# First x tiles on two load queues, and a new order of work within the first attention layer

## The chip, the cores and the metric

The kernel runs on one core of a Trainium2 chip. The metric is the device time of one execution in microseconds (us). The core has five engines that run their own instruction queues in order and meet only at semaphores: PE (TensorE, matrix multiply), DVE (VectorE), ACT (ScalarE), POOL (GpSimd) and SP (SyncE, which here only issues DMA transfers). ACT and POOL issue some transfers too.

## What is computed

Four blocks in a row on x, 2048 rows of 512 bf16 numbers: linear attention with 32 heads (layers 0 and 2) and a gated feed-forward block of width 1792 (layers 1 and 3), both with the same weights at their second use.

```python
def _A_ref(x, wqkv, wo):                      # H = 32, Dh = 16
    q, k, v = split_heads(x @ wqkv)
    phi = lambda t: jnp.where(t > 0, t + 1, jnp.exp(t)) + 1e-6
    pq, pk = phi(q), phi(k)
    kv = jnp.einsum("bhsd,bhse->bhde", pk, v)
    z = jnp.einsum("bhsd->bhd", pk)
    num = jnp.einsum("bhqd,bhde->bhqe", pq, kv)
    den = jnp.einsum("bhqd,bhd->bhq", pq, z)[..., None] + 1e-6
    return merge_heads(num / den) @ wo

def _B_ref(x, w_gate, w_up, w_down):
    return (silu(x @ w_gate) * (x @ w_up)) @ w_down

x = x + _A_ref(layernorm(x), wqkv, wo)
x = x + _B_ref(layernorm(x), w_gate, w_up, w_down)
x = x + _A_ref(layernorm(x), wqkv, wo)
x = x + _B_ref(layernorm(x), w_gate, w_up, w_down)
```

## The kernel before

The rows are cut into 16 tiles of 128 rows (x0 to x15), four to a group. Everything stays in SBUF. The order of the work is written out by hand: PROGRAM is the order of the steps, and with it the order of PE's instructions, and ORDER holds one list of operation names for each of the other engines. The class Prog keeps account of who wrote and read which buffer and sets the waits (`sync`, L65). A name is layer, step, tile, a dot and the kind of operation: `0x4.apply` is the application of the layer norm to tile 4 in layer 0, `0k0.exp` an operation of the projection of tile 0 to k. A number at the end counts operations of the same name on one engine (`0d3.pqn`, `0d3.pqn1`). The sets ON_ACT and ON_POOL say for some operations which engine does them.

The steps of layer 0, in the letters of PROGRAM:

- `S` is a matmul on zeros, without use for the result, which occupies PE until the first tile is there (L1250).
- `0x` (`ln`, L561) normalizes a tile. For most tiles DVE takes the statistics (stats L574, aggr L576); for tiles 2, 3, 6 and 14 ACT does (stats L581, sq L589) and POOL negates the mean (negm L593). Then vpe (L605, on POOL or DVE) and pow (L609, POOL) give 1/sqrt(var + eps); for tiles 11 and 14 ACT does that (rsl, rse, L599 and L601). The apply is on DVE (L620), or on ACT (L616), for which POOL first makes nmr (L613).
- `0t` (L632) transposes tiles 0 to 3 on PE, and ACT or DVE copies them out of PSUM (xT, L648, L651). Tiles 4 to 15 are transposed by DMA from SP's queue (xT, L629), one after the other.
- `0k` and `0q` project a tile (k) or a group (q, in four parts) with four matmuls of 512 columns, followed by phi (L660): ACT's exp (L664), for some also ACT's id1 (L667), and DVE's ts (L669) and phi (L673 where there is an id1, else L676).
- `0g` accumulates the products of k and the normalized x over all tiles in four pinned PSUM banks; `0z` sums k with matmuls of one column; `0d` forms the denominators and scales q by their reciprocals (pqn, L854). These are spread over a tile by a DMA transpose (rT, L844) of what ACT has repeated (rex, rep). In group 2 PE does it (`0r`).
- `0v` and `0m` form the matrices GT that `0w` multiplies with the scaled q, adding the result to x; after each `0w` DVE and others begin the layer norm of layer 1 for that tile.
- In layer 1, `1u` is a pair of projections (gate and up) with one SiLU, its product is named h. The Wd.tw operations between them subtract blocks of the down weights from each other.

PSUM has eight banks of 512 numbers per partition; a step takes the one that was used longest ago (`bank`, L448), if it isn't pinned.

All loads are issued by `dma` (L511). SP issues the first four tiles singly (ldx), then pairs of tiles (ldy), Wq (ldq) and Wv (ldv); ACT issues the two halves of Wk (ldk). The weights of later steps follow from POOL.

Of the kernel before, what the change touches and what calls it, by code (L numbers as in the profile page):

```python
# [192 lines left out]
1u001 1u006 1u012 1u011 0d33 1u004 1u005 1u013 1u003 1u008 1u002 1u010 1u113 1u101 1u009 0w13 1u110 0w14 1u104
1u105 0w15 0w12 1p01 1u102 1u107 1u112 1p05 1p06 1u103 1u108 1p07 1p02 1p04 1p03 1u111 1u100 1u109 1u106 1u213
1u206 1p11 1p15 1u208 1p16 1u210 1p17 1p12 1u207 1p14 1u203 1p13 2k0 2k1 1u303 1u209 2k2 1u204 1u212 2k4 1u205
1u202 1u201 1u211 1u302 1u309 2q01 2k3 1u200 1u310 1u306 1u313 1u308 1u301 1u304 2k6 2q10 1p21 2k5 1u305 1p26 1u307
1p27 1u300 1p22 1p25 1u311 1p24 1u312 1p23 1p31 1p35 2k7 1p36 1p33 1p37 2k11 2q02 1p34 1p32 2q12 2q00 2k9 2g11 2g2
2k10 2k8 2g7 2k15 2k14 2g10 2q11 2k13 2k12 2g9 2q31 2q20 2q21 2g13 2q13 2q03 2s 2g3 2g0 2d02 2d01 2d00 2d03 2g14
2d21 2g15 2q23 2d11 2g1 2q22 2g12 2g6 2d13 2d23 2g8 2g5 2d10 2d12 2g4 2d20 2d22 2q33 2v 2r1 2m3 2m1 2m2 2m0 2w3 2w2
2w0 2q32 2w1 2w6 2d31 2q30 2w4 2w8 2w7 2d32 2w10 2w9 2d33 2w11 2d30 2w5 3u001 3u010 3u004 3u008 3u005 3u000 3u002  # L200
2w12 2w15 3u009 2w14 2w13 3u011 3y105 3y101 3u012 3u003 3u006 3u007 3y111 3u112 3y115 3y106 3u105 3y116 3y102 3y107
3u013 3y104 3y103 3y121 3y112 3y117 3p01 3p05 3y113 3p06 3y125 3y114 3p02 3y131 3y126 3p07 3y132 3u106 3y136 3y122
# [15 lines left out]
0q20.exp 0q20.id1 0d0.rex2 0d1.ln 0G0.evac 0G2.evac 0G3.evac 0d1.rex1 0q30.exp 0d1.rex 0d2.ln 0d2.rxs 0q31.exp
0M0.evac 0q33.id1 0M1.evac 0M3.evac 0q33.exp 0d1.rex2 0d1.rex3 1x1.sq 1x2.sq 1x3.sq 1x2.apply 1x0.sq 0q32.id1
0q32.exp 1x0.apply 1x5.sq 1x4.sq 1x6.sq 1x11.sq 1x5.apply 1x7.sq 1u000.silu 1u007.silu 1x10.sq 1x8.sq 1u001.silu  # L220
1x9.sq 1u006.silu 1u012.silu 1u011.silu 1u004.silu 0d3.rep 0d3.rep1 1u005.silu 1u013.silu 1u003.silu 1u008.silu
1x11.apply 1u002.silu 1x9.apply 0d3.rep2 0d3.rep3 1u010.silu 1u113.silu 1u101.silu 1u009.silu 1u110.silu 1x13.sq
1u104.silu 1x14.sq 1x13.apply 1u105.silu 1x15.sq 1x12.sq 1u102.silu 1x15.apply 1x12.apply 1u107.silu 1u112.silu
1u103.silu 1u108.silu 2x2.sq 2x3.sq 1u111.tanh 2x1.sq 2x0.sq 1u100.tanh 2x2.apply 2x3.apply 1u109.tanh 2x1.apply
1u106.tanh 1u213.tanh 1u206.tanh 1u208.tanh 1u210.tanh 1u207.tanh 2x7.sq 1u203.tanh 2x6.sq 2x7.apply 2k0.exp 2x4.sq
1u303.tanh 2k1.exp 2x5.sq 1u209.tanh 2x6.apply 2k2.exp 2x5.apply 1u204.tanh 1u212.tanh 2k4.id1 2k4.exp 1u205.tanh
# [1143 lines left out]
```

## Time and profile before

| | |
|---|---|
| median of 3 runs | 410.11 us (409.76 to 410.12) |
| the profiled execution | 410.09 us, of which the span from the first to the last instruction is 408.3 us |
| PE busy | 397.8 us (97%) |
| DVE busy | 322.6 us (79%) |
| ACT busy | 245.2 us (60%) |
| POOL busy | 135.7 us (33%) |
| loads and stores | 23.29 MB moved, DMA engines busy 24% of the span |

Times in the profile are counted from the start of the span. The engines' names stand as above; SPq, ACTq and POOLq are the DMA-issuing instructions of an engine, PEld the weight loads of PE. An entry L469 is the line of the code that recorded the operation; all matmuls are recorded at one line, so they are told apart by what they read. Matmuls are pipelined: a group of them lasts longer than the distance to the start of the next.

### The profile page before, as it was taken

To read this page: it belongs to the slowest core of one execution; us is meant where nothing else is said; L and a number is where in the kernel's file an instruction comes from. 1 tells how busy PE (TensorE), PEld (TensorE's weight loads), DVE (VectorE), ACT (ScalarE), POOL (GpSimd) and SP (SyncE) were. 2 spreads that over 40 slices of the span, in tenths; PEclk is the share of its full clock that TensorE was granted. 3 is DMA by queue.
4 is the path that set the end of the run, shared out by engine and by line. 5 is a ranking of instruction groups with operands and counts; after the bars stand their busy time and mean duration, and the time that the engine had idled before them with its cause. 6 is when DMAs were issued, how large, how long until landed. Compare 5 with 4: busy or idle time off the path is not lost.

```text
span 408.3 us, 7311 instructions
## 1 busy us (share of the span) xinstructions
PE 397.8 (97%) x2673; PEld 244.2 (60%) x2714; DVE 322.6 (79%) x750; ACT 245.2 (60%) x492; POOL 135.7 (33%) x281
## 2 busy tenths in 40 slices
...
GB/s 274 141 101 270 197 52 90 195 60 46 51 2 40 13 1 53 0 2 0 2 27 30 50 2 61 83 65 81 49 27 0 44 12 0 53 2 0 2 54 51
DMA packets 53188, 23.29 MB, mean 57 GB/s; under 512 B 46432, under 2 KB 52064, under 8 KB 53152
## 3 DMA queue, kind: packets, MB, share of 16 engines
...
q10 hardware_dynamic: 544, 0.52, 0.4%
...
## 4 chain that ended last, share of the span: by engine, by line
PE 85%; ACT 6%; DVE 4%; DMA 2%; POOL 2%; issue 1%; SPq 0%; DVEq 0%; ACTq 0%
PE pb L469 85%; ACT etmp L664 1%; DMA RT<-rrep 1%; DMA X<-in_A_x_dram 1%; DVE X L884 1%; DVE pq L872 1%; ACT GT L758 1%; POOL rstd L609 1%; POOL Wqkv L975 1%; ACT tht L916 1%; DVE pk L676 0%; ACT pk L667 0%; ACT xnA L589 0%; ACT xnT L648 0%; POOL nmr L613 0%
## 5 line engine op out<-in xcount | busy, mean ns | idle before, releaser
L469 PE MATMUL pb<-xnT,Wu 128*128 128x512 bf16 (+1 forms) x383 | 95.0, 362 | 0.3
L469 PE MATMUL pb<-xnT,Wg 128*128 128x512 bf16 (+1 forms) x370 | 92.4, 362 | 0.9
L469 PEld LDWEIGHTS pb<-xnT,Wu 128*128 128x128 bf16 x388 | 38.0, 98 | 39.4
L469 PEld LDWEIGHTS pb<-xnT,Wg 128*128 128x128 bf16 x388 | 37.9, 98 | 34.3 <-DVE X L884 0.3
L918 DVE TENSOR_TENSOR hT<-tht,pb 128x512 bf16<-128x512 f32 x50 | 34.0, 683 | 22.1 <-PE pb L469 11.5
L664 ACT ACTIVATE etmp<-pb 128x512 bf16<-128x512 f32 x64 | 37.0, 597 | 14.4 <-PE pb L469 12.2
L916 ACT ACTIVATE tht<-pb 128x512 f32<-128x512 f32 x50 | 29.5, 594 | 26.8 <-PE pb L469 24.9
L1044 POOL TENSOR_TENSOR hT<-pq 128x256 bf16<-128x256 f32 x24 | 18.5, 778 | 76.9 <-ACT pq L1034 76.7
L907 ACT ACTIVATE tht<-pb 128x512 f32<-128x512 f32 x32 | 19.0, 595 | 35.4 <-PE pb L469 33.3
L469 PE MATMUL pb<-Wd,hT 128*128 128x256 bf16 x336 | 40.1, 273 | 0.0
L1049 ACT ACTIVATE pq<-pb 128x512 f32<-128x512 f32 x45 | 25.9, 595 | 22.6 <-PE pb L469 19.9
L593 POOL TENSOR_SCALAR mv<-sums 128x1 f32<-128x1 f32 x52 | 13.4, 267 | 75.8 <-DVE sums L1241 55.1
L609 POOL TENSOR_TENSOR rstd<-vpe,negh 128x1 f32<-128x1 f32 x62 | 36.0, 586 | 7.3 <-DVE vpe L605 4.2
L469 PEld LDWEIGHTS pb<-Wd,hT 128*128 128x128 bf16 x336 | 32.9, 98 | 5.7
L469 PE MATMUL pb<-Wqkv,xnT 128*128 128x512 bf16 x125 | 30.5, 379 | 2.7 <-ACT xnT L648 2.6
L1039 DVE TENSOR_TENSOR pq<-pb,pq 128x512 f32<-128x512 f32 x45 | 30.2, 684 | 3.3 <-ACT pq L1049 1.4
L469 PE MATMUL pb<-GT,pq 128*128 128x512 bf16 x125 | 30.1, 379 | 1.6 <-ACT GT L758 1.3
L469 PE MATMUL pb<-xnT,Wqkv 128*128 128x512 bf16 x122 | 30.9, 379 | 0.3
L469 PE MATMUL pb<-pk,xnA 128*128 128x512 bf16 x123 | 30.7, 378 | 0.3
L669 DVE TENSOR_SCALAR etmp<-etmp 128x512 bf16<-128x512 bf16 x64 | 18.4, 291 | 14.4 <-ACT etmp L664 14.0
L909 DVE SCALAR_TENSOR_TENSOR tht<-tht,pb 128x512 f32<-128x512 f32 x32 | 21.8, 684 | 6.1 <-ACT tht L907 5.9
L589 ACT ACTIVATE etmp<-X,sums 128x512 bf16<-128x512 bf16 x32 | 22.9, 716 | 4.1 <-DVE X L884 4.0
...
## 6 DMA issues: line engine op xcount, KB each, us to landing
out_dram<-pq SPq DMA_DIRECT2D x16, 128.0 KB, 1.8
...
Wd<-in_B_w_down_dram POOLq DMA_DIRECT2D x7, 256.0 KB, 4.5
X<-in_A_x_dram SPq DMA_DIRECT2D x6, 256.0 KB, 4.7
...
X<-in_A_x_dram SPq DMA_DIRECT2D x4, 128.0 KB, 3.5
Wqkv<-in_A_wqkv_dram ACTq DMA_DIRECT2D x2, 256.0 KB, 3.6
```

The costliest lines, as they stand in the source:

```text
L469: return op("pe", lambda e: e.matmul(o_ap, lhsT=lhsT, rhs=rhs, start=start, stop=stop, skip_group_check=skip), r=r, w=w, n=n)
L589: op("act", lambda a: a.activation(out=sq_ap, in_=X[:, t, :], func=ACT.Square, scale=-float(D), bias=sums[:, t:t + 1], accum_out=mv[:, t, ...
L609: op("pool", lambda p: p.tensor_tensor(out=rstd[:, t:t + 1], in0=vpe[:, t:t + 1], in1=negh[:], op=ALU.pow), r=[f"vp{t}", "negh"], w=[f"rs{ ...
L664: exps.append(op("act", lambda a: a.activation(out=etmp[e][:], in_=PB[pb], func=ACT.Exp), r=[f"pb{pb}"], w=[f"e{e}"], after=silus, kind="e ...
L669: op("dve", lambda v: v.tensor_scalar(out=etmp[e][:], in0=etmp[e][:], scalar1=1.0, scalar2=1e-6, op0=ALU.min, op1=ALU.add), r=[f"e{e}"], w ...
L907: op("act", lambda e: e.activation(out=tht[a][:], in_=PB[pg], func=ACT.Tanh, scale=0.5), r=[f"pb{pg}"], w=[f"th{a}"], kind="tanh")
L909: op("dve", lambda v: v.scalar_tensor_tensor(out=tht[a][:], in0=tht[a][:], scalar=1.0, in1=PB[pg], op0=ALU.add, op1=ALU.mult), r=[f"pb{pg} ...
L916: silus.append(op("act", lambda e: e.activation(out=tht[a][:], in_=PB[pg], func=ACT.Silu), r=[f"pb{pg}"], w=[f"th{a}"], after=exps, kind=" ...
L918: op("dve", lambda v: v.tensor_tensor(out=hT[h][:, j, :], in0=tht[a][:], in1=PB[pu], op=ALU.mult), r=[f"pb{pu}", f"th{a}"], w=hk, kind="h")
L1039: op("dve", lambda v: v.tensor_tensor(out=c, in0=PB[b], in1=c, op=ALU.add), r=[f"pb{b}", k], w=[k], kind="ca")
L1044: lambda e: e.tensor_tensor(out=hT[h][:, jj, o:o + 256], in0=c[:, 0:256], in1=c[:, 256:512], op=ALU.mult),
L1049: op("act", lambda e: e.activation(out=gs_tmp[3 * f + n], in_=PB[pb], func=ACT.Copy), r=pk_, w=[f"gt{3 * f + n}"], kind="cp")
```

## The change

Three things are changed. First, the loads of x1, x2 and Wk0 change queues: SP issues x0, x3 and Wk0, ACT issues x2, x1 and Wk1, in these orders. Second, the orders of all engines are written anew as far as the end of layer 0's attention, and with them some operations change engines: the applies of tiles 1 and 15 go from DVE to ACT and that of tile 4 from ACT to DVE; vpe of tile 8 goes from POOL to DVE; id1 of 0k8, 0k13 and 0q21 is left out (their phi takes the form without it) and 0q13 has one; G0 and G3 are evacuated by DVE instead of ACT, G1 by ACT instead of DVE. Third, one of the multiplies of group 3 (0d3, tile 1 of the group) goes from DVE to POOL, which stands where layer 1 has begun. After that the orders are as before. Other keys that leave ON_ACT are of operations that don't occur; `3s` in the code isn't in the set.

```diff
 PROGRAM = """
-S S S ... S 0t0 S 0k0 S S
-0t2 0t1 0t3 0k2 0k1 0k3 0q00 0q03 0g0 0g2 0g1 0g3 0k4 0k9 0q01 0k10 0k5 0g4 0z2 0g9 0z1 0k6 0z3 0z10 0q12 0k7 0k13
-0k15 0k14 0g5 0z5 0q13 0g6 0z6 0z9 0z13 0q11 0z14 0k8 0k11 0z7 0q02 0q23 0z0 0k12 0z11 0z4 0z15 0g8 0q22 0z12 0z8
-0q21 0d03 0d00 0d02 0d01 0g10 0q10 0d13 0g12 0g14 0g11 0q20 0d10 0d11 0d21 0g15 0d12 0g7 0d23 0g13 0d22 0q30 0d20
-0v 0q31 0m0 0q33 0m2 0m3 0m1 0w1 0w2 0w3 0d30 0r2 0w0 0w5 0q32 0w4 0d31
+S S S ... S S 0t0 0t2 0k0
+0t3 S 0k2 0t1 0k3 S 0k1 0q03 0q00 0g2 0g3 0g0 0k4 0g1 0k9 0q01 0k10 0k5 0g4 0z2 0g9 0z1 0k6 0z3 0z10 0q12 0k7 0k13
+0k15 0k14 0g5 0z5 0q13 0g6 0z9 0q11 0z14 0z13 0k8 0z6 0k11 0z7 0q02 0q23 0k12 0z4 0z11 0z15 0g8 0q22 0z12 0z8 0z0 0q21
+0d03 0d02 0d01 0d00 0g10 0g12 0q10 0d13 0d21 0g11 0q20 0d10 0d11 0g14 0g15 0d12 0g7 0d23 0g13 0d22 0d20 0q30 0v 0q31
+0m0 0q33 0m3 0m2 0m1 0w1 0w2 0w3 0d30 0r2 0w0 0w5 0w4 0q32 0d31
...
     "act": """
-i.ldk i.ldk1 0x2.stats 0x2.sq 0x3.stats 0x3.sq 0t0.xT 0k0.exp 0t2.xT 0t1.xT 0k0.id1 0x4.apply 0k2.exp 0k1.exp 0x6.stats 0k3.exp
-0q00.id1 0q00.exp 0x5.apply 0q03.exp 0x6.sq 0x14.stats 0x14.sq 0x7.apply 0k4.id1 0k4.exp 0k9.exp 0x14.rsl 0q01.exp
+i.ldx1 i.ldx i.ldk 0x2.stats 0x2.sq 0x3.stats 0x3.sq 0t0.xT 0t2.xT 0x1.apply 0k0.exp 0k0.id1 0t1.xT 0k2.exp 0k3.exp
+0x6.stats 0x14.stats 0k1.exp 0x6.sq 0x14.sq 0q03.exp 0q00.exp 0q00.id1 0x5.apply 0k4.exp 0k4.id1 0x7.apply 0x14.rsl
+0x14.rse 0k9.exp 0q01.exp 0x15.apply 0k10.exp 0k10.id1 0k5.exp 0x11.rsl 0x14.apply 0x8.apply 0k6.exp 0x11.rse 0q12.id1
...
     "dve": """
-i.c 0x0.stats 0x0.aggr 0x0.apply 0x1.stats 0x2.vpe 0x1.aggr 0x1.vpe 0x3.vpe 0x2.apply 0x4.stats 0x1.apply 0x3.apply
-0x4.aggr 0x9.stats 0x10.stats 0x9.aggr 0t3.xT 0k0.ts 0x5.stats 0k0.phi 0x9.apply 0x10.aggr 0x5.aggr 0k2.ts 0x7.stats
-0k1.ts 0k2.phi 0x10.apply 0k3.ts 0k1.phi 0k3.phi 0q00.ts 0x7.aggr 0x13.stats 0q00.phi 0x13.aggr 0q03.ts 0x15.stats
-0q03.phi 0x15.aggr 0x6.apply 0x11.stats 0x13.apply 0x8.stats 0k4.ts 0x15.apply 0k9.ts 0k4.phi 0k9.phi 0q01.ts
+i.c 0x0.stats 0x0.aggr 0x1.stats 0x2.vpe 0x0.apply 0x1.aggr 0x1.vpe 0x2.apply 0x3.vpe 0x4.stats 0x3.apply 0x9.stats
+0x4.aggr 0x9.aggr 0t3.xT 0x7.stats 0x10.stats 0k0.ts 0x5.stats 0k0.phi 0k2.ts 0x5.aggr 0k3.ts 0x4.apply 0x10.aggr
+0k2.phi 0k3.phi 0x7.aggr 0x9.apply 0k1.ts 0k1.phi 0x10.apply 0q03.ts 0x15.stats 0q03.phi 0x13.stats 0q00.ts 0x15.aggr
+0x13.aggr 0x6.apply 0q00.phi 0k4.ts 0x8.stats 0x11.stats 0x8.aggr 0k9.ts 0k4.phi 0q01.ts 0x11.aggr 0x8.vpe 0k9.phi
...
-1u010.h 1u113.h Wd.tw5 Wd.tw7 1x10.apply 1u101.h 0d3.pqn2 1x8.apply 0d3.pqn3 1u009.h 1h0.sb 0w13.res 1h0.sa 1h0.sb3
...
+0d3.pqn1 1u010.h 1u113.h Wd.tw5 Wd.tw7 1x10.apply 1u101.h 0d3.pqn2 1x8.apply 1u009.h 1h0.sb 0w13.res 1h0.sa 1h0.sb3
...
     "pool": """
-i.c5 i.c i.c2 i.c6 i.c1 i.c4 i.c3 i.c7 i.c8 i.c9 0x0.vpe 0x0.pow 0x2.negm 0x3.negm 0x2.pow 0x1.pow 0x3.pow 0x4.vpe
+i.c7 i.c i.c5 i.c8 i.c4 i.c6 0x0.vpe 0x2.negm 0x0.pow i.c1 0x2.pow 0x3.negm 0x1.pow 0x3.pow 0x1.nmr i.c2 i.c3 0x4.vpe
...
-1x9.pow 1x11.pow 1x9.nmr 1x10.vpe 1x10.negm 1x10.pow 1x8.vpe 1x11.nmr 1x8.pow Wd.tw2 1x8.negm Wd.tw3 Wd.tw Wd.tw1
+1x9.pow 1x11.pow 1x9.nmr 1x10.vpe 1x10.negm 1x10.pow 1x8.vpe 1x11.nmr 1x8.pow Wd.tw2 1x8.negm Wd.tw3 Wd.tw 0d3.pqn
...
     "sp": """
-i.ldx i.ldx2 i.ldx3 i.ldx1 i.ldy i.ldy2 i.ldy3 i.ldy1 i.ldq i.ldy5 i.ldy4 i.ldv 0x4.xT 0x9.xT 0x10.xT
-0x5.xT 0x6.xT 0x7.xT 0x15.xT 0x13.xT 0x14.xT 0x8.xT 0x11.xT 0x12.xT 0d0.rT1 0d0.rT 0d0.rT3 0d0.rT2 0d1.rT1 0d1.rT
+i.ldx i.ldx1 i.ldk i.ldy i.ldy2 i.ldy3 i.ldy1 i.ldq i.ldy5 i.ldy4 i.ldv 0x4.xT 0x9.xT 0x10.xT 0x5.xT 0x6.xT 0x7.xT
+0x15.xT 0x13.xT 0x14.xT 0x8.xT 0x12.xT 0x11.xT 0d0.rT1 0d0.rT 0d0.rT3 0d0.rT2 0d1.rT1 0d1.rT 0d1.rT2 0d1.rT3 1x1.xT
...
 ON_POOL = set("""
-0d0.2 0d0.3 2d0.2 2d0.3
+0d0.2 0d0.3 0d3.1 2d0.2 2d0.3
 """.split())
...
         for t in range(TG):
-            dma("sp", X[:, t, :], x2d[t * P:(t + 1) * P, :], w=[f"x{t}"], kind="ldx")
+            dma("act" if f"0a{t}" in ON_ACT else "sp", X[:, t, :], x2d[t * P:(t + 1) * P, :], w=[f"x{t}"], kind="ldx")
         for c in range(2):
-            dma("act", Wqkv[:, 2 * c:2 * c + 2, D:2 * D], wq3[:, 2 * c:2 * c + 2, D:2 * D], w=[f"Wk{c}"], kind="ldk")
+            dma("sp" if f"0b{c}" in ON_ACT else "act", Wqkv[:, 2 * c:2 * c + 2, D:2 * D], wq3[:, 2 * c:2 * c + 2, D:2 * D], w=[f"Wk{c}"], kind="ldk")
```

In ON_ACT after the change stand, of the keys that count here, 0a1, 0a2, 0b0, 0p8, 0q13, 0x1, 0x15, 0G1; 0G0, 0G3, 0k8, 0k13, 0q21, 0x4 are gone.

## Rows read from the trace of the kernel before

**Rows 1.** The page: busy us, share of the span, instructions.
```profile
PE 397.8 (97%) x2673; PEld 244.2 (60%) x2714; DVE 322.6 (79%) x750; ACT 245.2 (60%) x492; POOL 135.7 (33%) x281
```

**Rows 2.** Waits of PE, whole span: us in total, times, longest.
```profile
PE pb L469 <- ACT xnT L648: 2.6, 2, 2.2
PE pb L469 <- ACT GT L758: 1.3, 2, 0.8
```

**Rows 3.** Timeline of PE: start us, us, operation, count, idle before and releaser.
```profile
5.74 0.40 PE L643 MATMUL pb<-ident,xnA 128*128 128x128 bf16 x4
...
8.38 0.81 PE L469 MATMUL pb<-Wqkv,xnT 128*128 128x512 bf16 x3 [2.19 <-ACT xnT L648]
...
9.13 0.83 PE L643 MATMUL pb<-ident,xnA 128*128 128x128 bf16 x12
10.36 2.76 PE L469 MATMUL pb<-Wqkv,xnT 128*128 128x512 bf16 x12 [0.40 <-ACT xnT L648]
...
18.14 1.89 PE L469 MATMUL pb<-Wqkv,xnT 128*128 128x512 bf16 x8
...
55.73 2.60 PE L469 MATMUL pb<-GT,pq 128*128 128x512 bf16 x11 [0.47 <-ACT GT L758]
```

**Rows 4.** Timeline of ACT, 4 to 12 us.
```profile
4.51 0.63 ACT L581 ACTIVATE xnA<-X 128x512 bf16<-128x512 bf16 x1 [2.44 <-DMA X<-in_A_x_dram]
...
7.44 0.57 ACT L648 ACTIVATE xnT<-pb 128x512 bf16<-128x512 bf16 x1
9.22 0.60 ACT L664 ACTIVATE etmp<-pb 128x512 bf16<-128x512 f32 x1 [1.21 <-PE pb L469]
...
10.67 0.70 ACT L667 ACTIVATE pk<-pb,onep 128x512 bf16<-128x512 f32 x1
11.24 0.83 ACT L616 ACTIVATE xnA<-X,nmr,rstd 128x512 bf16<-128x512 bf16 x1
```

**Rows 5.** Timeline: the first DMA issues of SP and of ACT.
```profile
0.79 3.83 SPq L512 DMA_DIRECT2D X<-in_A_x_dram  x8
0.81 0.96 ACTq L512 DMA_DIRECT2D Wqkv<-in_A_wqkv_dram  x2
```

**Rows 6.** DMA, stretches of single issues (x0, Wk0, x2, x1; tiles 4, 9): us to landing.
```profile
X<-in_A_x_dram SPq DMA_DIRECT2D x1, 128.0 KB, 2.6
Wqkv<-in_A_wqkv_dram ACTq DMA_DIRECT2D x1, 256.0 KB, 3.3
...
X<-in_A_x_dram SPq DMA_DIRECT2D x1, 128.0 KB, 3.2
...
X<-in_A_x_dram SPq DMA_DIRECT2D x1, 128.0 KB, 3.8
...
xnT<-xnA SPq DMA_TRANSPOSE x1, 3.4
...
xnT<-xnA SPq DMA_TRANSPOSE x2, 3.0
```

**Rows 7.** Timeline of DVE, 12 to 14 us.
```profile
11.98 0.40 DVE L620 TENSOR_SCALAR xnA<-X,mv,rstd 128x512 bf16<-128x512 bf16 x1
...
13.61 0.68 DVE L676 SCALAR_TENSOR_TENSOR pk<-pb,etmp 128x512 bf16<-128x512 f32 x1
```

**Rows 8.** Windows, 10.4 to 26 us: busy PE, PEld, DVE, ACT, POOL; clock, DMA.
```profile
10.40:26.00 15.60, 15.47 (x85) 7.32 (x88) 15.23 (x46) 15.19 (x33) 8.43 (x24) 1.00 0.57 126
```

**Rows 9.** Timeline, 83 to 97 us, where layer 1 has begun.
```profile
83.18 5.46 POOL L553 TENSOR_TENSOR Td<-Wd,Td 128x512 bf16<-128x512 bf16 x5
...
90.30 3.40 SPq L844 DMA_TRANSPOSE RT<-rrep  x2
90.42 0.75 DVE L854 TENSOR_TENSOR pq<-pq,RT 128x512 bf16<-128x512 bf16 x2
...
96.12 1.03 PE L469 MATMUL pb<-xnT,Wg 128*128 128x512 bf16 x4
```

**Rows 10.** DMA, the RT transpose issued at 90.30: us to landing.
```profile
RT<-rrep SPq DMA_TRANSPOSE x1, 3.2
```

More of the change, by code (lines that the diff above doesn't have):

```diff
@@ L193 @@
[L193 to L202, printed above, removed]
@@ L209 @@
+3y336 3y335 3p26 3y332 3y327 3y337 3p22 3y323 3u313 3p27 3y333 3y324 3y341 3y345 3p24 3y346 3y342 3y334 3y347 3p23
+3y343 3y344 3p31 3p32 3p35 3p36 3p33 3p37 3p34
 """
@@ L218 @@
[L218 to L226, printed above, removed]
-1u202.tanh 1u201.tanh 1u211.tanh 1u302.tanh 1u309.tanh 2q01.exp 2q01.id1 2k3.id1 2k3.exp 1u200.tanh 1u310.tanh
@@ L249 @@
+3y333.sih 3y346.cp 3y334.sih 3y347.cp 3y342.sih 3y347.sih 3y344.sih 3y343.sih
 """,
     "dve": """
[L251 to L254 removed]
```

164 lines of the change are left out of this document (88 added, 76 removed).

## The prediction, made before the changed kernel was run

> **What bounds the kernel now.** I read the page's engine shares first, then PE's waits, then the timeline of the first 26 us engine by engine, and the issues of the first loads. PE is busy 397.8 of 408.3 us, 97% [rows 1], so only time in which PE has nothing to do can be won. Once it works, PE waits for another engine's data almost nowhere: 2.6 us in two waits for a transposed tile that ACT copies out of PSUM, and 1.3 us in two for GT [rows 2]; one of these two GT waits lies at the end of the first attention layer and one in layer 2. The reader should see in rows 3 that both tile waits are at the very start: PE transposes tile 0 at 5.74, stands still for 2.19 us, begins 0k0 at 8.38, and stands still for another 0.40 us before 0k2 at 10.36. From there on one group follows the other without a gap: twelve 512-column matmuls take 2.76, eight take 1.89, so four cost 0.865 us. So this kernel is a start of some 10 us and then PE at its rate; a microsecond saved in the start lasts to the end if no later stage makes PE wait, and whatever PE waits later is lost.
>
> What sets 8.38: PE waits for ACT's 0t0.xT at 7.44 [rows 4]. PE had finished the transposes before 6.2; ACT was not free. Its queue holds 0x2.stats, 0x2.sq, 0x3.stats, 0x3.sq ahead of that copy, begun at 4.51, after 2.44 us of waiting for tile x2 [rows 4]. So x2's landing sets 0k0: 8.38 - 4.51 = 3.87 us from landing to first projection. x2 is the second transfer on SP's queue: eight issues take 3.83 us there, 0.48 each [rows 5], so it goes out at 1.27, and lands 3.2 us later [rows 6].
>
> **The change, part by part.** *Loads.* SP now issues x0, x3, Wk0 and ACT x2, x1, Wk1. x2 becomes the first transfer of its queue, 128 KB at 0.81 instead of 1.27. What such a one takes is bounded by two rows: x0, first on SP with 128 KB, 2.6 us; Wk0, first on ACT with 256 KB, 3.3 us [rows 6]. So x2 lands between 3.4 and 4.1, and I take 3.4 because x0 is the same size in the same place. That is 1.1 us earlier (0.4 at the other end). x3 and x1 become second in their queues, like x2 before: about 4.5 (1.27 + 3.2); as fourth transfer x1 landed at 6.0 (3.8 us after its issue at 2.2 [rows 6]). x3 is in time for ACT, which reaches it 1.5 us after x2. The price is Wk: Wk0 and Wk1 now stand where x3 and x1 stood, with the same bytes ahead of each queue's end, so they land by about 6.0. 0k0 needs them at 7.3; the cover is 1.3 us and I cost this at nothing. Later transfers on SP go one issue earlier with the same bytes ahead and I leave them where they were. The Trainium skill speaks against this part: "DMA: Bandwidth & Descriptors", section "Rules for kernel authors", says that spreading DMAs over issuing engines brings no bandwidth, since they share the same DMA engines, and only saves issue time. By that rule alone x2 would gain its issue slot and no more.
>
> *ACT's start.* The four statistics operations still stand ahead of 0t0.xT, so 0k0 comes 3.87 us after x2: 3.4 + 3.9 = 7.3 instead of 8.38, a gain of 1.1. 0x0.apply moves behind 0x1.stats and 0x2.vpe on DVE, and on POOL 0x2.negm goes ahead of 0x0.pow; this delays 0x0.apply, and with it the transposes that began at 5.74 [rows 3], by some 0.3 us, to about 6.0, and ACT is free for the copy at 3.4 + 2.9 = 6.3, so this costs nothing (cover 0.2 to 0.3 us).
>
> *The order on PE.* 0t2 goes ahead of 0k0, then 0t3, 0k2, 0t1, 0k3, 0k1. Each tile's copy is thus made while another tile is projected. The 0.40 us in front of 0k2 [rows 3] goes: another gain of 0.4, with the copy of tile 2 done at about 7.6 and 0k2 due at 8.4. One more spin matmul ahead of 0t0 costs nothing, because PE waits for 0x0.apply there.
>
> *What is late next.* Between 0k0 and the first tile of the second group, 0k4, PE now has four k, two q and three g (0g1 goes behind 0k4): 9 x 0.865 = 7.8 us, and 0.5 of transposes (twelve take 0.83 [rows 3]), so 0k4 is due at 7.3 + 8.3 = 15.6, against 18.14 before [rows 3]. Its tile comes by DMA. 0x4.apply leaves ACT (11.24 [rows 4]) for DVE, where it is queued behind 0k2.ts and 0k3.ts; 0k3.ts waits for ACT's 0k3.exp, and that for PE's 0k3, which ends at 7.3 + 3 x 0.865 + 0.5 = 10.4. With ACT's queue (0k2.exp before it, about 0.6 each [rows 4]) the exp ends at 11.3, and the apply at about 12.1. SP's transpose behind it took 3.4 us for tile 4 [rows 6]: 15.5. Cover of 2.6 us before, of 0.1 after. Tile 9 is alike: 0x9.apply, at 11.98 before, moves behind 0k2.phi and 0k3.phi, 0.68 us each [rows 7], to about 13.7; its transpose took 3.0 [rows 6], 16.8, and 0k9 is due at 17.4. I give back 0.2 us here, between nothing and the 0.9 that a DVE late by 1.0 us would cost.
>
> *DVE and ACT from 10 to 26 us* are nearly as full as PE: 15.23 and 15.19 of 15.60 us [rows 8]. DVE loses two applies and gains one and a small vpe (-0.3 us), ACT gains two of 0.83 and loses one (+0.8), and two of 0.70 (0k13.id1, 0k8.id1) leave it after 26 us [rows 4], where DVE takes the 0.68 us form of phi for them. Both engines also begin earlier by about 1 us, since x2 and x1 land earlier. So they can keep up with a PE that is 1.1 to 1.5 us ahead, but with nothing to spare.
>
> *The tail of the layer.* z, d and g steps change places, two evacuations of G go from ACT to DVE. PE's amount of work is the same; the wait for GT before 0w1 stays, as M1 and M3 are still copied by ACT after the last m step. Nothing.
>
> *0d3.1 on POOL.* This reaches into the next layer. The multiply of tile 1 moves to POOL behind two Wd.tw of 1.1 us each (five in 5.46 [rows 9]); that ends by 87, and 0w13, its reader, comes one group before the 96.12 of rows 9. On DVE the second of the two multiplies at 90.42 [rows 9] is now that of tile 2, whose RT transpose is issued at 90.30 [rows 9] and lands 3.2 us later [rows 10], at 93.5. DVE, free at 90.8, waits 2.7 us, with 1u010.h (right behind these two multiplies) and all others queued behind it; 1u010.h ends at 94.6. Who waits for that is PE, when the rotation of eight PSUM banks comes to the bank that this step reads: that is 1u110's gate half, at 96.12 [rows 9]. Cover 1.5 us; the banks after it come later still. So nothing, unless the wait exceeds 2.7 + 1.5 = 4.2 us.
>
> **The sum.** The profiled execution took 410.09 us, 1.8 around a span of 408.3; the median of the runs is 410.11, the same. -1.1 - 0.4 + 0.2 = -1.3: 408.8.
>
> **The rivals.** *Issue time only.* If the two queues share so that x2 wins only its slot of 0.48 us, 0k0 gains 0.5: -0.5 - 0.4 + 0.2, 409.4. For it: of equal tiles the later ones took longer, 2.6, 3.2 and 3.8 us [rows 6], so the loads share something. Against it: x0, alike, lands after 2.6. This is the rule cited above. *The second group's tiles come late.* If DVE runs 1 us behind my account, 0k4 and 0k9 wait, and 1.5 shrinks to about 0.5: 409.6. For it: no cover, DVE full. Against it: DVE's own start is earlier. *Slower: the same chain, worse.* 0x4.apply now depends on x1's branch (POOL's nmr, ACT's 0x1.apply, PE's 0t1 ahead of 0k3), where before it came right behind 0k0.id1 on ACT. Each us by which 0x4.apply ends after 12.2 is a us of waiting at 0k4; from 2.3 us late, 14.5, the kernel is more than 0.8 us slower: 411.0. Against it: every step of that branch has some tenths of cover in my account, none needs 2 us. *The loads do nothing*, as if ACT's issue waited for its table load: only the 0.4, 409.7. Against it: ACT issued its two at 0.81 before [rows 5]. *More than I think:* no loss at 0k4 and x2 a little earlier still, 408.1.
>
> **How the numbers follow.** Forecast 408.8 (408.4 to 409.2) 0.52; more 0.10; issue time only 0.13, of which 0.05 below the bound; late tiles 0.13; loads do nothing 0.04; slower 0.08. A measurement of this kernel can tell 0.2%, 0.8 us, from no change: 409.3 and 410.9 are the bounds. Faster 0.52 + 0.10 + 0.05 = 0.67; same 0.08 + 0.13 + 0.04 = 0.25; slower 0.08. The range 408.0 to 410.0 leaves out the slower case and the ends.
>
> **What the profile after would show.** ACT's first statistics at 3.4 (right), 4.0 (issue time only) or 4.5; 0k0 at 7.3; no idle PE before 0k2; PE without a wait at 0k4, near 15.6, and 0k9; DVE idle some 2.7 us near 89 with no wait of PE near 95; all of layers 1 to 3 shifted by 1.3 us. I am wrong if PE waits for a transposed tile of the second group, or if a stage from 12 us on opens a gap that was not there.

## The result, and the profile after

The changed kernel takes 413.29 us, median of 7 runs (411.63 to 415.92), beside 409.77 for the kernel before on the same chip: a ratio of 1.0086, 95% interval 1.0070 to 1.0102. It is slower by 3.5 us, where 1.3 us less was forecast. The profiled execution is the fastest of the 7: 411.63 with a span of 409.9, so its trace shows 1.6 us of the loss and not the larger part that most runs have; the experiments below show at which place that arises. The mean granted clock of PE was 1.0 in the five runs up to 413.39 and 0.996 and 0.995 in the two longest, so the 3.5 us of the median are no matter of the clock. In the code of after, line numbers are 5 lower than before (L464 is the matmul helper).

The waits of PE over the whole span (us in total, times, longest), which answer to [rows 2]:

```profile
PE pb L464 <- ACT GT L753: 1.3, 2, 0.8
...
PE pb L464 <- DVE pq L668: 1.2, 1, 1.2
PE pb L464 <- ACT xnT L643: 0.7, 1, 0.7
PE pb L464 <- DVE pk L671: 0.3, 1, 0.3
```

The waits for a copied tile fell from 2.6 to 0.7 us. Two are new: 1.2 us for DVE's pq (a phi of q) and 0.3 us for pk. The timeline of PE tells where:

```profile
6.40 0.70 PE L638 MATMUL pb<-ident,xnA 128*128 128x128 bf16 x8
7.78 0.81 PE L464 MATMUL pb<-Wqkv,xnT 128*128 128x512 bf16 x3 [0.68 <-ACT xnT L643]
...
11.83 1.89 PE L464 MATMUL pb<-xnT,Wqkv 128*128 128x512 bf16 x8
...
25.84 1.04 PE L464 MATMUL pb<-Wqkv,xnT 128*128 128x512 bf16 x4
27.19 2.75 PE L464 MATMUL pb<-Wqkv,xnT 128*128 128x512 bf16 x12 [0.32 <-DVE pk L671]
29.78 1.03 PE L464 MATMUL pb<-pk,xnA 128*128 128x512 bf16 x4
...
50.22 0.24 PE L464 MATMUL pb<-Zm,pq 128*128 128x8 bf16 x4
51.70 0.26 PE L464 MATMUL pb<-Zm,pq 128*128 128x8 bf16 x4 [1.24 <-DVE pq L668]
...
57.08 1.09 PE L464 MATMUL pb<-GT,pq 128*128 128x512 bf16 x4 [0.47 <-ACT GT L753]
```

The same steps of the kernel before (behind the four k; 0k7 and the three k after it; 0g5):

```profile
12.96 1.89 PE L469 MATMUL pb<-xnT,Wqkv 128*128 128x512 bf16 x8
...
26.31 3.68 PE L469 MATMUL pb<-Wqkv,xnT 128*128 128x512 bf16 x16
29.83 1.03 PE L469 MATMUL pb<-pk,xnA 128*128 128x512 bf16 x4
```

0k0 starts at 7.78 instead of 8.38 [rows 3], 0.6 us earlier, and the step behind the four k at 11.83 instead of 12.96, 1.13 us earlier. At 0k7 only 0.47 us of that are left (25.84 against 26.31): PE loses the rest in short gaps that the list of waits does not name and that were not followed up. At 27.19, in front of 0k13, PE waits; 0k7 ahead of it began at 25.84 and its four matmuls take 0.87, so 0.5 us are lost there. The g step at 29.78 was at 29.83 before: the whole gain is gone by 30 us. At 51.70, in front of 0d20, PE waits 1.24 us, and the GT wait that stood at 55.73 [rows 3] stands at 57.08: 1.35 us late. It stays about 1.5 us late to the end.

What DVE does ahead of that wait (timeline, start us, us, operation, idle before and releaser):

```profile
46.20 0.42 DVE L668 TENSOR_TENSOR pq<-pq,etmp 128x512 bf16<-128x512 bf16 x1
49.02 0.42 DVE L849 TENSOR_TENSOR pq<-pq,RT 128x512 bf16<-128x512 bf16 x1 [2.40 <-DMA RT<-rrep]
49.37 0.29 DVE L664 TENSOR_SCALAR etmp<-etmp 128x512 bf16<-128x512 bf16 x1
50.88 0.43 DVE L849 TENSOR_TENSOR pq<-pq,RT 128x512 bf16<-128x512 bf16 x1 [1.23 <-DMA RT<-rrep]
51.23 0.42 DVE L668 TENSOR_TENSOR pq<-pq,etmp 128x512 bf16<-128x512 bf16 x1
51.56 1.28 DVE L756 CAST GT<-pb 128x512 bf16<-128x512 f32 x2
```

Before, DVE stood 1.72 us at the same place:

```profile
47.53 0.98 DVE L854 TENSOR_TENSOR pq<-pq,RT 128x512 bf16<-128x512 bf16 x2 [1.72 <-DMA RT<-rrep]
```

The lines L849 are 0d0.pqn1 and 0d0.pqn, which multiply by RT, the reciprocals that SP spreads over a tile by a DMA transpose. DVE stands 3.6 us for the two transposes; behind them in its queue are 0q20.phi (51.23), for which 0d20 waits, and the two copies of G (51.56), for which 0v waits. The transposes are late because they take longer. DMA from 43 to 50 us, issues and median us to landing, first of after, then of before:

```profile
Wg<-in_B_w_gate_dram POOLq DMA_DIRECT2D x1, 448.0 KB, 5.5
RT<-rrep SPq DMA_TRANSPOSE x2, 5.5
RT<-hT SPq DMA_TRANSPOSE x2, 3.7
```

```profile
RT<-rrep SPq DMA_TRANSPOSE x2, 3.4
RT<-hT SPq DMA_TRANSPOSE x2, 3.4
```

SP issues them at the same time in both (43.84 and 43.79). What differs is POOL's last weight load, a Wg: it goes out inside this stretch in after, 0.81 us ahead of the transposes, and at 42.20 before, 1.59 us ahead. The timeline of POOL in after, then the last load before:

```profile
41.89 0.54 POOL L507 DMA_DIRECT2D Wg<-in_B_w_gate_dram  x1 [0.59 <-DMA Wg<-in_B_w_gate_dram]
43.03 0.54 POOL L507 DMA_DIRECT2D Wg<-in_B_w_gate_dram  x1 [0.60 <-DMA Wu<-in_B_w_up_dram]
```

```profile
42.20 0.54 POOL L512 DMA_DIRECT2D Wg<-in_B_w_gate_dram  x1 [0.59 <-DMA Wu<-in_B_w_up_dram]
```

### The profile page after: what moved, and what is told of

The parts are those of the page before. It is cut to its first block, busy times and chain, and to the rows that moved or that the text cites. A ratio compares the mean times of both kernels' runs of the same rounds, so it can differ in the third digit from the quotient of the medians.

```text
span 409.9 us, 7311 instructions
## 1 busy us (share of the span) xinstructions
PE 399.3 (97%) x2673; PEld 244.4 (60%) x2714; DVE 323.3 (79%) x750; ACT 245.1 (60%) x490; POOL 137.8 (34%) x282
## 4 chain that ended last, share of the span: by engine, by line
PE 87%; DVE 4%; ACT 3%; DMA 3%; issue 1%; POOL 1%; SPq 0%; DVEq 0%; ACTq 0%
PE pb L464 87%; DMA RT<-rrep 1%; DMA X<-in_A_x_dram 1%; ACT etmp L659 1%; DVE stats L569 1%; ACT GT L753 1%; DVE pq L1226 1%; POOL rstd L604 0%; DVE etmp L664 0%; ACT xnA L611 0%; DVE xnA L1156 0%; ACT pq L662 0%; DVE pk L671 0%; DVE pq L1034 0%; SPq L507 0%
## 5 line engine op out<-in xcount | busy, mean ns | idle before, releaser
L464 PE MATMUL pb<-xnT,Wu 128*128 128x512 bf16 (+1 forms) x383 | 95.0, 362 | 0.3
L464 PE MATMUL pb<-xnT,Wg 128*128 128x512 bf16 (+1 forms) x370 | 92.4, 362 | 1.0
L464 PEld LDWEIGHTS pb<-xnT,Wu 128*128 128x128 bf16 x388 | 38.0, 98 | 39.4
L464 PEld LDWEIGHTS pb<-xnT,Wg 128*128 128x128 bf16 x388 | 37.8, 98 | 34.5 <-issue 0.7
L464 PE MATMUL pb<-Wd,hT 128*128 128x256 bf16 x336 | 40.1, 273 | 0.0
L1044 ACT ACTIVATE pq<-pb 128x512 f32<-128x512 f32 x45 | 26.0, 595 | 22.6 <-PE pb L464 19.8
L464 PEld LDWEIGHTS pb<-Wd,hT 128*128 128x128 bf16 x336 | 32.9, 98 | 5.7
L464 PE MATMUL pb<-Wqkv,xnT 128*128 128x512 bf16 x124 | 30.8, 379 | 1.2 <-ACT xnT L643 0.7
L464 PE MATMUL pb<-xnT,Wqkv 128*128 128x512 bf16 x123 | 31.1, 379 | 0.3
L464 PE MATMUL pb<-GT,pq 128*128 128x512 bf16 x125 | 29.8, 379 | 1.5 <-ACT GT L753 1.3
L464 PE MATMUL pb<-pk,xnA 128*128 128x512 bf16 x123 | 30.5, 378 | 0.4
```

The lines of the kernel that those rows point to most:

```text
L464: return op("pe", lambda e: e.matmul(o_ap, lhsT=lhsT, rhs=rhs, start=start, stop=stop, skip_group_check=skip), r=r, w=w, n=n)
L1044: op("act", lambda e: e.activation(out=gs_tmp[3 * f + n], in_=PB[pb], func=ACT.Copy), r=pk_, w=[f"gt{3 * f + n}"], kind="cp")
```

## The experiments

My theory after this reading (A): weight loads that move beside the transposes into RT make these slow, DVE waits for them in order, and PE waits for what is queued behind. Rivals: the loads at the start make runs late by themselves (C); the new orders of the engines lose by themselves (B). Each median is of 4 to 12 runs, and each ratio is to the kernel before on the same chip (409.78 to 409.92).

| run | what it is | median us | ratio to before, 95% |
|---|---|---|---|
| after_again | the changed kernel | 413.43 | 1.0089 (1.0071 to 1.0108) |
| free_dve | 0q20 and G ahead of RT on DVE | 411.11 | 1.0031 (1.0019 to 1.0043) |
| d20_late | 0d20 back behind 0q30 | 414.28 | 1.0103 (1.0083 to 1.0122) |
| loads_only | new loads, old orders | 410.42 | 1.0036 (1.0010 to 1.0063) |
| orders_only | old loads, new orders | 413.79 | 1.0095 (1.0072 to 1.0119) |
| weights_later | changed, three weight loads later | 413.57 | 1.0086 (1.0072 to 1.0099) |
| loads_weights | loads_only, three weight loads later | 413.19 | 1.0076 (1.0064 to 1.0089) |
| mended | three edits at once | 413.77 | 1.0095 (1.0079 to 1.0110) |
| after_between2 | changed, two weight loads held | 410.93 | 1.0022 (1.0012 to 1.0032) |
| loads_between2 | loads_only, two held | 409.50 | 0.9991 (0.9982 to 1.0000) |
| loads_between2_b | the same again | 409.75 | 0.9994 (0.9985 to 1.0002) |
| loads_between3 | loads_only, three held | 410.32 | 1.0010 (1.0001 to 1.0019) |
| x2_between2 | only x2 on ACT, two held | 409.63 | 0.9993 (0.9984 to 1.0001) |
| before_between2 | before, two held | 409.72 | 0.9994 (0.9985 to 1.0003) |
| after_x3_first | after_between2, x3's apply first | 411.14 | 1.0025 (1.0014 to 1.0036) |
| after_x4_act | after_between2, x4's apply on ACT | 410.89 | 1.0023 (1.0013 to 1.0033) |
| after_x15_dve | after_between2, x15's apply on DVE | 409.94 | 0.9998 (0.9987 to 1.0009) |
| after_three | after_x15_dve, two more edits | 410.12 | 1.0008 (0.9999 to 1.0017) |

### DVE's place behind RT

**after_again**, no edit.

> The changed kernel itself, once more, to see how its time spreads and whether the wait of 1.24 us in front of 0d20 has the same length in another execution. If this wait is a wait for DMA transposes that meet the weight loads (theory A), it should differ from execution to execution and make the spread of 411.6 to 415.9 us. If the loss comes from the orders alone (theory B: DVE and ACT too full from 13 to 30 us), the wait is the same each time, near 1.2 us.

413.43: the same again. In its profile (412.10) the wait at 0d20 is 0.62 us, but this does not tell A from B: DVE is done with the phi at nearly the same time as in after, and the wait is shorter because PE comes there 0.8 us later.

**free_dve**:

```diff
 DVE
-0d0.pqn1 0q20.ts 0d0.pqn 0q20.phi 0G0.evac 0G3.evac
+0q20.ts 0q20.phi 0G0.evac 0G3.evac 0d0.pqn1 0d0.pqn
```

> On DVE 0q20.ts, 0q20.phi, 0G0.evac and 0G3.evac go ahead of the two multiplies 0d0.pqn1 and 0d0.pqn, which wait for the RT transposes. Theory A (0d20 and then 0v wait for DVE, which waits for the transposes): the wait of 1.24 us in front of 0d20 goes, 0v starts near 51.3 as in the kernel before, and the time falls by 1.2 us or more, to 410 us or less, with a small spread. Theory B (the layer is late anyway): PE waits as long for something else, and the time stays at 412 to 413 us.

411.11, with all runs within 1.3 us. The wait at 0d20 is gone. Of 3.6 us lost, 2.3 were in this one place of DVE's queue. The forecast of 410 or less missed: 1.3 us lie elsewhere.

**d20_late**, PE's order `0q30 0d20 0v` instead of `0d20 0q30 0v`:

> On PE only, 0d20 goes back behind 0q30. Theory A: the 0.86 us of 0q30 cover a part of the wait, but 0v still needs 0G0 and 0G3, which DVE copies behind the same multiplies: gain of 0.3 to 0.9 us against the changed kernel, and PE then waits in front of 0v. If the place of 0d20 alone were the fault, the gain would be the whole 1.24 us.

414.28: no better, so the gain that was expected did not come. Another step in front of 0d20 doesn't help, since 0v waits for DVE as well. The profiled execution took 415.18 us, the second longest of the six, and so shows what the profile of after, the fastest execution, doesn't. The transposes took a median of 6.6 us; DVE waited 4.8. Busy time and granted clock of PE in stretches of 2 us (columns: stretch, its length, busy with count, clock, DMA share, GB/s), and two rows of its timeline:

```profile
52.00:54.00 2.00, 0.46 (x6) 1.00 0.35 69
54.00:56.00 2.00, 1.40 (x14) 0.67 0.64 128
56.00:58.00 2.00, 1.78 (x8) 0.50 0.00 0
58.00:60.00 2.00, 2.00 (x10) 0.97 0.00 0
```

```profile
53.76 0.26 PE L464 MATMUL pb<-Zm,pq 128*128 128x8 bf16 x4 [1.54 <-DVE pq L668]
...
56.75 1.48 PE L464 MATMUL pb<-xnT,Wqkv 128*128 128x512 bf16 x3 [0.22 <-issue]
```

PE was busy 0.46 of 2 us, and after that the granted clock went to 0.50, the lower of its two levels (1.2 of 2.4 GHz), until 58. Three matmuls that take 0.81 us at full clock took 1.48. So a wait can cost more than itself. It does not always: the last section has waits of like length without a fall of the clock.

### The weight loads beside the transposes

**loads_only**, the kernel before with:

```diff
 ACT
-i.ldk i.ldk1 0x2.stats
+i.ldx1 i.ldx i.ldk 0x2.stats
 SP
-i.ldx i.ldx2 i.ldx3 i.ldx1 i.ldy
+i.ldx i.ldx1 i.ldk i.ldy
```

> The kernel before with the new loads alone: x2, x1 and Wk1 from ACT, x0, x3 and Wk0 from SP, all orders else as before. My account: x2 lands at 3.7 as in the changed kernel instead of 4.5, 0k0 starts 0.6 to 0.8 us earlier than 8.38, and as PE waits nowhere later in the kernel before, 0.4 to 0.8 us of it last to the end: 409.0 to 409.4 us. Rival: the gain is lost at 0t0.xT or in front of 0k2, and the time is that of the kernel before.

410.42, from 409.04 to 415.13. Missed as well. The profiled one has a span of 408.1 and no wait for RT on PE, though the transposes took 5.1 us there and DVE stood 3.44 us for them: in that execution the old order hid the wait. The long runs have no profile. So the new loads alone, with DVE's old order, spread the times up to where the changed kernel's lie.

**orders_only**, the changed kernel with the old loads (the diff above backwards):

> The changed kernel with the loads of before (SP: x0, x2, x3, x1; ACT: Wk0, Wk1), so the new orders alone. x1 lands near 6.0 and DVE's 0x1.stats now stands ahead of 0x0.apply: the first transposes at 7.2 instead of 6.4 and 0k0 at 8.6 to 9.0. Theory (the new orders lose by themselves, at 0k13 and behind 0d0.pqn on DVE): 412 to 414. Rival (it is the earlier loads that upset the weight loads and RT, the orders are harmless): RT lands in 3 to 4 us, no wait at 0d20, 410 to 411.

413.79. PE waited 2.43 us at 0d20 behind RT here too (profiled execution 415.14, the longest of four), with the clock at 0.50 after it. The orders lose with either loads. With the old loads SP's pairs of tiles took a median of 4.7 us, as before, and RT still took 6.4: POOL's last load went out at 44.10, 0.33 us ahead of the transposes.

**weights_later** (the changed kernel) and **loads_weights** (loads_only), each with:

```diff
 POOL
-i.ld6 i.ld7 i.ld5 0d0.pqn1 0d0.pqn
+0d0.pqn1 0d0.pqn i.ld6 i.ld7 i.ld5
```

> The changed kernel, with one edit: the last three weight loads that POOL issues (the last Wu and two of Wg, out at 40.8, 41.9 and 43.0 us in its profile) go behind POOL's two pqn multiplies of step 0d0, so to about 54 us. Theory A (the transposes into RT, issued at 43.8, take 5.2 to 7 us because these three loads are still moving beside them): they land within 2.5 to 3.5 us, DVE's wait for RT falls from 3.6 to 1.5 us or less, PE has no wait at 0d20, and with the clock never falling the time is as with DVE freed, 410.8 to 411.3, with a spread below 1.5 us. Theory B (the transposes are slow by themselves, since they are issued later or stand behind others of SP's queue): they take 5 us and more again, PE waits 0.6 us or more at 0d20, 413.0 to 413.6. If the loads are missed where they are now late, layer 1 waits for Wg or Wu near 69 us: that would show as a wait of PE there.

> The kernel before with the new loads alone (x2, x1, Wk1 on ACT; x0, x3, Wk0 on SP), as in the run of the loads alone, and with the same last three weight loads of POOL behind its multiplies of 0d0. The loads alone gave 410.4 with runs from 409.0 to 415.1. Theory A (what spread them is the transposes into RT, late because the weight loads move at that time): median 408.9 to 409.3, no run above 410. Theory C (the spread comes from the start, x and Wk now landing late in some runs): median 410.2 again and some runs at 413 or more.

Both times missed, 413.57 and 413.19, but both profiles bear A out. In weights_later the first pair of transposes, from 43 to 50 us, took this:

```profile
RT<-rrep SPq DMA_TRANSPOSE x2, 2.4
RT<-hT SPq DMA_TRANSPOSE x2, 3.2
```

2.4 us instead of 5.5, no wait at 0d20, and 0v at 50.94 against 51.40 before. But the loads now go out at 52.8 to 54.4, beside the second pair (issued from 51.55), and the wait returned there, with w1's addition (L879) queued on DVE behind 0d1's multiply and PE's attention outputs waiting for it:

```profile
58.76 0.42 DVE L849 TENSOR_TENSOR pq<-pq,RT 128x512 bf16<-128x512 bf16 x1 [2.88 <-DMA RT<-rrep]
59.10 0.68 DVE L879 SCALAR_TENSOR_TENSOR X<-pb,X 128x512 bf16<-128x512 f32 x1
```

```profile
59.85 2.79 PE L464 MATMUL pb<-GT,pq 128*128 128x512 bf16 x12 [1.55 <-DVE X L879]
```

In loads_weights PE's wait at this place is 2.90 us. The wait follows the loads. **mended** had these later loads too, with the DVE edit of free_dve, and 0x15.apply on ACT moved from ahead of 0k10.exp to behind 0k10.id1:

> The changed kernel with three edits: 0q20.ts, 0q20.phi and the two evacuations of G ahead of 0d0.pqn1 on DVE; the last three weight loads behind 0d0.pqn on POOL; 0x15.apply on ACT behind 0k10.id1 instead of ahead of 0k10.exp, where ACT stood 0.78 us for it at 21.6. Theory: DVE freed gave 411.1; the third edit closes PE's 0.3 us at 0k13 (27.2) and gives up to 0.5 more: 410.4 to 410.8, not yet faster than before, since DVE and ACT are full from 16 to 28 us. Rival (the gain at the start was only lost at 0k13 and at 0d20): with both closed the kernel keeps the 0.6 to 1.1 us of the start and takes 408.8 to 409.3.

413.77, above both forecasts: the same wait near 60 us. The move of 0x15.apply also failed: 0k13 waited 0.43 us for a transposed tile instead.

So the loads were put between the two pairs. In **loads_between2**, **after_between2**, **x2_between2** and **before_between2** two loads wait for the second of the first pair; in **loads_between3** i.ld6 too:

```diff
+        for n in ("i.ld7", "i.ld5"):
+            named["pool", n].deps.add(named["sp", "0d0.rT"].i)
         pr.schedule()
```

> The kernel before with the new loads of the start, in the old order of every engine, and with the last two weight loads of POOL (two of Wg) made to wait for the second of the first pair of RT<-rrep transposes, so that they go out near 46.5 us, behind that pair and ahead of the next pair at 51. Theory A (the gain of the new loads at the start is real, 0.5 to 1.1 us at 0k0, and nothing but weight loads moving beside transposes into RT takes it back): both pairs land in 2.5 to 4 us, no wait of PE at 0d20 or before the attention outputs near 60, 408.7 to 409.4, faster than before. Theory C (runs of this load order start late by themselves): 410 or more, with runs at 413.

> The changed kernel with the last two weight loads held back in the same way. Theory A (of the change's loss, all but the share of the orders comes from RT): RT<-rrep in 2.5 to 4 us, no wait of 0.5 us or more at 0d20; of the start's gain 0.46 us was left at 0v where no RT wait was in the way, so 409.3 to 409.8, the same as before, 3.5 us less than the changed kernel. If the new orders cost something else in the later part, it shows here as more than 410.2 without a wait for RT.

> As the run with two loads held back, but with the last three (the last Wu too). The first pair of RT<-rrep now lands beside nothing, the second pair, out near 51, may meet the tail of the third load: 1.34 MB at the 335 to 420 GB/s that the same weights moved at between 36 and 40 us is 3.2 to 4 us, so they are in by 52 or so. Theory A: 408.7 to 409.6; if DVE waits for RT near 56 to 59 with w1's addition queued behind, PE waits there and it is 410 to 411.

409.50, 410.93 and 410.32; the first two are above what theory A gave (by 0.1 and by 1.1 us). The transposes take 2.5 to 2.7 us (medians of the two first runs), and nothing on PE waits for them by more than 0.2 us. The spread goes as well: loads_only's highest time falls from 415.13 to 410.38, the changed kernel's from 415.92 to 411.69. That speaks against C. Two quite different edits, DVE's order (411.11) and the held loads (410.93), agree on what RT cost: 2.3 to 2.5 us (by the ratios, 2.3 to 2.7). Three held loads are one too many: PE waits 1.0 us for POOL's multiply (L854) at 57.44.

**x2_between2** leaves both Wk on ACT and moves x2 alone there; **before_between2** is the control; **loads_between2_b** repeats the best.

> As the kernel before with the new loads and two weight loads held back, but with x2 alone moved to ACT: SP x0, x3, x1, then the pairs; ACT x2, Wk0, Wk1. Theory: x2's place at the head of a queue is what gives 0k0, and with both Wk on ACT the tiles x4 and x5 stay one place earlier on SP and Wk0 lands earlier: 0k0 between 7.2 and 7.8, as with the full change of loads, and 408.6 to 409.4. Rival (x1 behind x3 on SP lands late and 0k1's tile with it): PE waits for 0t1, 409.5 to 410.

> The kernel before, loads and orders untouched, with the last two weight loads of POOL held back behind the first pair of RT<-rrep. Theory (the 0.4 us won with the new loads was theirs, from an earlier 0k0; before has no wait for RT on PE that holding back could remove): 409.7 to 410.0, the same as before. Rival (the holding back is what won): 409.4 to 409.6.

> The same kernel as the first run with the new loads, old orders and two weight loads held back (409.50, 0.9991 of before), again. 0k0 begins 7.2 to 8.1 us into the span in the profiles of these loads, against 8.38 before, and in the old orders 0k7 follows 17.9 to 18.2 us behind it every time. Theory: 409.3 to 409.6 again, with runs from 409.0 to 410.4 as x2 and Wk0 land earlier or later. If it is 409.8 or more the first result was chance.

409.63, 409.72, 409.75: only the control came as forecast, and none differs from before by what can be told here. The new loads with the old orders win 0.1 to 0.4 us at most, and holding the loads back in the kernel before comes out 0.2 us lower without them. A likely reason is in the start of these profiles: 0k0 comes anywhere from 7.21 (loads_weights) to 8.06. In two of these six profiles it was late for Wk, as in loads_between2_b (timeline of PE):

```profile
8.06 1.04 PE L469 MATMUL pb<-Wqkv,xnT 128*128 128x512 bf16 x4 [1.84 <-DMA Wqkv<-in_A_wqkv_dram]
```

### What the orders lose

after_between2 minus loads_between2 is 1.4 us: the same loads, no RT wait, only the orders differ, with the operations that changed engines. In nine profiles of the new orders 0k13 began 19.3 to 19.8 us after x4's statistics, whatever 0k0 did. Three edits, one at a time, each on after_between2:

```diff
 after_x3_first, DVE
-0x4.stats 0x3.apply
+0x3.apply 0x4.stats
 after_x4_act: 0x4.apply from DVE to ACT
-0t1.xT 0k2.exp 0k3.exp
+0t1.xT 0k2.exp 0x4.apply 0k3.exp
 after_x15_dve: 0x15.apply from ACT to DVE, without its nmr on POOL
-0k9.ts 0k4.phi 0q01.ts 0x11.aggr
+0k9.ts 0k4.phi 0q01.ts 0x15.apply 0x11.aggr
```

> The changed kernel with the last two weight loads held back (410.93 so) and one place changed on DVE: 0x3.apply ahead of 0x4.stats, so that it no longer waits for x4. In the profiles of the new orders 0x4.stats begins at 7.6 to 8.7 us, as x4 lands, and 0k13 begins 19.3 to 19.7 us after it, whatever 0k0 did (7.4 to 8.3). Theory D (DVE is full from x4's landing to 0k13, so only what DVE does before that counts): the wait at 0t3 is gone, 0k13 comes 19.2 to 19.3 us after 0x4.stats, 0.4 us sooner, and the time is 410.4 to 410.6. Rival E (the late 0t3 itself is what shifts all that follows, 0.8 us): 0k13 follows 0k0 instead, 19.3 us after it or less, and the time is 409.8 to 410.2.

411.14, 0k13 19.6 us after x4. The wait at 0t3 went, and PE waited 0.40 us for that tile's copy and 0.48 us for phi instead: nothing won.

> The changed kernel with the last two weight loads held back (410.93) and 0x4.apply back on ACT, ahead of 0k3.exp (with its small nmr step on POOL), instead of on DVE behind 0k3.ts. Theory F (the new orders lose at the front because x4's apply is queued late on DVE; SP's transposes of the second group, POOL's weights behind them and 0k13 all follow it): SP's first transpose comes 4.2 to 4.8 us after 0x4.stats instead of 5.5, 0k13 some 0.7 to 1.2 us sooner after it (18.4 to 19.0), and the time is 409.9 to 410.4. Rival (the front is bound by DVE and ACT as a whole, whichever of them has x4's apply): SP's transposes begin sooner, 0k13 is still 19.3 to 19.7 us after 0x4.stats, 410.8 to 411.2.

410.89. SP's first transpose came 4.45 us after x4's statistics instead of 5.5, 0k13 19.8: theory F fell.

> The changed kernel with the last two weight loads held back (410.93) and 0x15.apply back on DVE, behind 0q01.ts, where it needs no nmr step of POOL. Theory G (ACT's wait of 0.8 us for that nmr, handed on to DVE and to PE at 0k13, is half of what the orders lose): no wait of ACT near 22 us, 0k13 comes 18.7 to 19.1 us after 0x4.stats instead of 19.6, and the time is 410.1 to 410.5. Rival (DVE and ACT are full in this order, so 0.4 us more on DVE and the same tile late give it back): 0k13 19.4 us or more after 0x4.stats, 410.8 to 411.1.

409.94, 1.0 us less. The rows of after_between2, ACT, then DVE, then PE:

```profile
22.78 0.81 ACT L611 ACTIVATE xnA<-X,nmr,rstd 128x512 bf16<-128x512 bf16 x1 [0.86 <-POOL nmr L608]
```

```profile
25.17 0.29 DVE L664 TENSOR_SCALAR etmp<-etmp 128x512 bf16<-128x512 bf16 x1 [0.71 <-ACT etmp L659]
```

```profile
28.41 1.89 PE L464 MATMUL pb<-Wqkv,xnT 128*128 128x512 bf16 x8 [0.32 <-DVE pk L671]
```

and PE in after_x15_dve, where sixteen matmuls from 0k7 on run without a wait, and 0k13 is 18.9 us behind x4 (26.53 + 0.87 - 8.53):

```profile
26.53 3.68 PE L464 MATMUL pb<-Wqkv,xnT 128*128 128x512 bf16 x16
```

0x15.apply on ACT waits 0.8 us for a small step that POOL reaches late; the exps queued behind it come late, DVE waits for them, and the bank that 0k13 needs comes free late. On DVE the apply needs no such step. The edit takes the 0.81 us of the apply itself off ACT as well; how much of the 1.0 us is the wait and how much the work was not told apart. **after_three** adds to this the edits of after_x3_first and free_dve:

> The changed kernel with the last two weight loads held back and 0x15.apply on DVE (409.94 so far), and now 0x3.apply ahead of 0x4.stats and 0q20.ts, 0q20.phi and the two evacuations of G ahead of 0d0.pqn1 on DVE. Theory (0t3's wait of 0.84 us is the remainder): 409.2 to 409.6, faster than before by the part of the start's gain that the landing of Wk0 leaves. Rival (DVE is full after x4's landing, so what is won at 0t3 is given back at the next k): 409.8 to 410.2, the same as before, as x3's apply first alone won nothing.

410.12: the rival holds, nothing more is won. Its profiled execution is the fastest of 11 (409.32, 0k0 at 7.48); that is no gain of the median. The 0.2 to 0.6 us that lie between these two kernels and the old orders with the same loads are not settled.

## Why the prediction was wrong, step by step

**The tail of the layer: "Nothing".** This is the step that failed. I counted PE's work and which engine copies G, and not DVE's queue. Behind the multiplies that wait for RT stood 0q20.phi and one copy of G before too, and DVE waited 1.72 us there; but 0d20, the reader of that phi, came behind 0q30 on PE, and nothing was due. The change moves 0d20 ahead of 0q30, gives DVE two copies of G that ACT made before, and the wait grew to 3.6 us. It cost 2.3 us (free_dve), 2.4 with the loads held (after_between2). The place of 0d20 alone is not it, since d20_late puts that back and is no faster; whether the copies of G alone would do was not tested.

**"Later transfers on SP ... I left them where they were."** Wrong. SP's six pairs of tiles took a median of 4.7 us before and 6.0 after. x4's statistics waited 0.67 us for it, the second group's transposes began at 13.08 instead of 12.09 and POOL's weights, which wait for the last of them, at 32.13 instead of 31.32. So the last load came closer to the transposes into RT. But the later pairs are not needed for that. With the old loads and the new orders (orders_only) the pairs took 4.7 us, the second group's transposes began at 13.55 and the last load met RT all the same; with the new loads and the old orders (loads_only) these transposes began at 11.78, and the last load still went out at 42.72, 0.66 us ahead of RT. Either half of the change brings the two together; why in loads_only is open.

**"x2 lands between 3.4 and 4.1, I take 3.4."** Right within its bounds: 3.73 here, 3.36 to 3.76 in the profiles of all runs with x2 at the head of ACT's queue.

**Wk "by about 6.0 ... cover 1.3 us, nothing".** Mis-sized: Wk0 and Wk1 took 4.9 and 5.4 us where 3.6 was the median before, so they came at about 6.6 and 7.1. In after that was just in time; in six of the experiments' profiles 0k0 waited for them, by 0.66 to 1.90 us. What x2 gained, Wk paid. That is the rule that I set against this part, from the Trainium skill, "DMA: Bandwidth & Descriptors", section "Rules for kernel authors": more issuing engines bring no more bandwidth. The traces agree in the main: x2 came 0.8 us earlier, 0.3 more than its slot of 0.48, while Wk and the pairs took 1.3 us longer or more.

**0k0 at 7.3, and 0.4 at 0k2.** 7.78; 0.3 of the 0.5 us that it came late is x2's landing. The 0.4 us was won: the four k ended at 11.83 instead of 12.96, 1.13 us of gain, at 12 us.

**DVE and ACT "can keep up, but with nothing to spare".** Wrong by 1.0 us (after_x15_dve). I counted 0x15.apply on ACT as 0.83 us of work that it could hold; ACT also stands 0.8 us for POOL's nmr in front of it. The row of work was there, the wait that it brings along was not asked for.

**The second group's tiles.** 0x4.apply ended at 13.05 (12.1 in my account) and 0k4 came at 16.37 (15.6), without a wait of PE for its tile, so my sign of being wrong there did not show; after_x4_act, where SP's first transpose comes 1 us sooner and the time stays, shows that this was not the loss. The slower rival named a real weakness, but not the one that decided.

**0d3.1 on POOL.** Right. DVE waits 3.2 us for tile 2's transpose (2.7 forecast) until 95.24, and no PE wait follows:

```profile
95.24 0.43 DVE L849 TENSOR_TENSOR pq<-pq,RT 128x512 bf16<-128x512 bf16 x1 [3.20 <-DMA RT<-rrep]
```

**The chances.** 0.08 for slower was too little, since each rival was a place that I had looked at. The layer's tail, which has the only other PE wait of [rows 3] in this layer, I had not followed engine by engine.

**What the two steps add up to.** With the loads held and 0x15.apply on DVE the kernel takes 409.94 (0.9998), the time of the kernel before. So the layer's tail and 0x15.apply make up the loss against before, and the 1.3 us that I had forecast are missing besides: the new loads win 0.1 to 0.4 us in the old orders, and the new orders lose what they win at 12 us by 30 us.
